# A hand-ordered rewrite of a gated attention and MLP backward pass: 4-byte transposes, long weight rows, program order

## The chip, the cores and the metric

The kernel runs on one core of a Trainium2 chip. The metric is the device time of one execution in microseconds (us). One execution of each kernel was also profiled. In what follows PE is TensorE (PEld are its weight loads), DVE is VectorE, ACT is ScalarE, POOL is GpSimd, SP is SyncE, which here issues the loads and, at the end, a few small stores. PEclk is the share of the full TensorE clock that was granted. L472 is a line of the kernel whose profile is being read, so the same operation has different line numbers in different kernels.

A run counts as slow if it is over 1.5% above the fastest of the same kernel, and the recorded ratios are formed from fast runs. The medians beside them are over all runs of a kernel. The profiled execution of the kernel before is not one of the listed ones: its span of 459.0 us is longer than that of every run of it that the record lists as fast (448 to 456 us), so small differences from its profile mean nothing.

## The reference, cut to what matters

The program computes a forward pass and all its gradients: a decode-size attention block (one query token, 32 heads, a cache of 4096 keys of 128 numbers) and a small MLP (640 to 1728 to 640), mixed by a sigmoid gate.

```python
q = (x @ wq).reshape(B, 1, 32, 128).transpose(0, 2, 1, 3)
scores = einsum("bhqd,bhkd->bhqk", q, k_cache) * 128 ** -0.5
p = softmax(scores)
o = einsum("bhqk,bhkd->bhqd", p, v_cache)
a = o.transpose(...).reshape(B, 1, 4096) @ wo
h = x @ w1 + b1;  b = (h * tanh(softplus(h))) @ w2
out = g * a + (1 - g) * b          # g = sigmoid(sum(x * gate_w))
# returned: out and the gradients of x, k_cache, v_cache, wq, wo, w1, b1, w2, gate_w
```

For each head the kernel reads 1 MB of K and 1 MB of V and writes 1 MB of dK and 1 MB of dV. dV is the outer product of p with the output gradient row, and dK is the outer product of ds with q, where `ds = p * (dp - sum(p * dp))` and dp is V times the output gradient. All in all about 165 MB pass between HBM and the chip. With only one query, the arithmetic is light: most of the work is to transpose K and V so that TensorE can multiply them, and to write the outer products.

## The kernel before: the parts that the argument touches

Each head transposes 32 blocks of K and 32 of V, 128x128 in bf16, eight to a PSUM tile, copies them out on ACT and multiplies them by a vector. The work is written head by head. A scheduler then orders the instructions of every engine, with `high_priority` marking the short dependent chain.

```python
def transposes(src, dst):
    for c in range(NTB):
        tp = tr_ps.tile([P, TB, P], BF16, name="tr", tag="tr")
        for t in range(TB):
            nc.tensor.transpose(tp[:, t, :], src[:, c * TB + t, :], ident_bf[:])
        nc.scalar.copy(...)                                  # 128x512 as float32
KT = kvT.tile([P, J, P], BF16, name="KT", tag="KT")
transposes(Kn, KT)
for j in range(J):
    nc.tensor.matmul(S[:, j:j + 1], lhsT=KT[:, j, :], rhs=gp["qTs_g"][:, hh:hh + 1], ...)
with hp():                                                   # tc.high_priority
    ...                                                      # max, exp, sum, 1/sum, p
... # the same for V, then ds, dq, o, and the outer products dV and dK
```

wo and wq are transposed on PE as well. wo rows are 1280 bytes, wq pieces 1024 bytes, and dwq is written group by group in 1024-byte pieces.

Of the kernel before, what the change touches and what calls it, by code (L numbers as in the profile page):

```python
# [8 lines left out]
ALU = mybir.AluOpType  # L9
# [7 lines left out]
def kernel(  # L17
# [29 lines left out]
    assert Dh == P and Sk % P == 0 and D % P == 0  # L47
    J = Sk // P
    RC = D // P
    G = 4 if H % 4 == 0 else (2 if H % 2 == 0 else 1)  # L50
    NG = H // G
    GD = G * Dh
    FP = 96
    assert F % FP == 0
    FCN = F // FP
    FCC = 3 if FCN % 3 == 0 else 1
    NCH = FCN // FCC
    FW = FCC * FP
    scale = float(Dh) ** -0.5
    TB = 8 if J % 8 == 0 else J  # L60
    NTB = J // TB
    JD = max(1, min(J - 1, int(round(J * 0.59)))) if J > 1 else J
# [7 lines left out]
    wo_v = A_wo.rearrange("(h d) n -> d h n", d=P)  # L70
    dwo_v = out_5.rearrange("(h d) n -> d h n", d=P)
    w1_v = B_w1.rearrange("(rc r) f -> r rc f", r=P)
    dw1_v = out_6.rearrange("(rc r) f -> r rc f", r=P)
    w2_v = B_w2.rearrange("(fc p) n -> p fc n", p=FP)
    dw2_v = out_8.rearrange("(fc p) n -> p fc n", p=FP)
    b1_row = B_b1.rearrange("(o f) -> o f", o=1)
    db1_rows = out_7.rearrange("(fc p) -> fc p", p=FP)
    x_row = A_x.rearrange("a b d -> (a b) d")
    x_rows = A_x.rearrange("a b (c p) -> (a b c) p", p=P)
    dy_row = grad_out.rearrange("a b d -> (a b) d")  # L80
    dy_rows = grad_out.rearrange("a b (c p) -> (a b c) p", p=P)
    gw_row = gate_w.rearrange("(o d) -> o d", o=1)
# [4 lines left out]

    const = ctx.enter_context(tc.tile_pool(name="const", bufs=1))
    KBUFS, VBUFS = 4, 4
    kv_in = ctx.enter_context(tc.tile_pool(name="kv_in", bufs=KBUFS))  # L90
    kvT = ctx.enter_context(tc.tile_pool(name="kvT", bufs=1))
    outs = ctx.enter_context(tc.tile_pool(name="outs", bufs=3))
    wts2 = ctx.enter_context(tc.tile_pool(name="wts2", bufs=2))
    wts1 = ctx.enter_context(tc.tile_pool(name="wts1", bufs=1))
    small = ctx.enter_context(tc.tile_pool(name="small", bufs=4))
    mlp1 = ctx.enter_context(tc.tile_pool(name="mlp1", bufs=1))
    tr_ps = ctx.enter_context(tc.tile_pool(name="tr_ps", bufs=2, space=PSUM))
    ss_ps = ctx.enter_context(tc.tile_pool(name="ss_ps", bufs=3, space=PSUM))
    grp_ps = ctx.enter_context(tc.tile_pool(name="grp_ps", bufs=2, space=PSUM))
    qd_ps = ctx.enter_context(tc.tile_pool(name="qd_ps", bufs=1, space=PSUM))  # L100
    HP = 1200
    LP = -200000

    def f32view(ap2d):
        return ap2d.bitcast(F32)

    ident_bf = const.tile([P, P], BF16, name="ident_bf")
    nc.gpsimd.memset(ident_bf[:], 0.0)
    nc.gpsimd.affine_select(
        out=ident_bf[:], in_=ident_bf[:], compare_op=ALU.not_equal, fill=1.0,  # L110
# [4 lines left out]
    ones_f = const.tile([P, P], F32, name="ones_f")  # L115
    nc.vector.memset(ones_f[:], 1.0)
    zeros_f = const.tile([P, 32], F32, name="zeros_f")
    nc.vector.memset(zeros_f[:], 0.0)
    warm = const.tile([P, 8], F32, name="warm")
    nc.gpsimd.tensor_tensor(warm[:], zeros_f[:, 0:8], zeros_f[:, 8:16], ALU.add)  # L120

    with tc.tile_pool(name="setup", bufs=1) as sp:
        vec_rows = sp.tile([3 * RC, P], BF16, name="vec_rows")
        nc.scalar.dma_start(vec_rows[0:RC, :], x_rows)
        nc.scalar.dma_start(vec_rows[RC:2 * RC, :], dy_rows)
        nc.scalar.dma_start(vec_rows[2 * RC:3 * RC, :], gw_rows)
        xg_bc = sp.tile([P, 2, D], BF16, name="xg_bc")
        nc.scalar.dma_start(xg_bc[:, 0, :], x_row.partition_broadcast(P))
        nc.scalar.dma_start(xg_bc[:, 1, :], gw_row.partition_broadcast(P))
        dy_bc = sp.tile([P, D], BF16, name="dy_bc")  # L130
        nc.scalar.dma_start(dy_bc[:], dy_row.partition_broadcast(P))

        cols_ps = grp_ps.tile([P, 3 * RC], BF16, name="cols_ps", tag="grp")
        nc.tensor.transpose(cols_ps[:], vec_rows[:], ident_bf[0:3 * RC, 0:3 * RC])
        cols_bf = const.tile([P, 3 * RC], BF16, name="cols_bf")
        nc.scalar.copy(cols_bf[:], cols_ps[:])
        cols_f = const.tile([P, 3 * RC], F32, name="cols_f")
        nc.vector.tensor_copy(cols_f[:], cols_ps[:])
        x_col_bf = cols_bf[:, 0:RC]
        x_col_f = cols_f[:, 0:RC]  # L140
        dy_col_f = cols_f[:, RC:2 * RC]
        gw_col_f = cols_f[:, 2 * RC:3 * RC]

        zprod = sp.tile([P, D], F32, name="zprod")
        nc.vector.tensor_tensor(zprod[:], xg_bc[:, 0, :], xg_bc[:, 1, :], ALU.mult)
        z_all = sp.tile([P, 1], F32, name="z_all")
        nc.vector.reduce_sum(z_all[:], zprod[:], axis=AX.X)
        en = sp.tile([P, 1], F32, name="en")
        nc.scalar.activation(en[:], z_all[:], ACT.Exp, scale=-1.0)
        den = sp.tile([P, 1], F32, name="den")  # L150
        nc.vector.tensor_tensor(den[:], en[:], ones_f[:, 0:1], ALU.add)
        g_raw = sp.tile([P, 1], F32, name="g_raw")
        nc.vector.reciprocal(g_raw[:], den[:])
        g_bf = sp.tile([P, 1], BF16, name="g_bf")
        nc.vector.tensor_copy(g_bf[:], g_raw[:])
        g_all = const.tile([P, 1], F32, name="g_all")
        nc.vector.tensor_copy(g_all[:], g_bf[:])
        omg_bf = sp.tile([P, 1], BF16, name="omg_bf")
        nc.vector.tensor_tensor(omg_bf[:], ones_f[:, 0:1], g_all[:], ALU.subtract)
        omg_all = const.tile([P, 1], F32, name="omg_all")  # L160
        nc.vector.tensor_copy(omg_all[:], omg_bf[:])

        da_col_bf = const.tile([P, RC], BF16, name="da_col_bf")
        nc.vector.tensor_tensor(da_col_bf[:], dy_col_f, g_all[:].to_broadcast([P, RC]), ALU.mult)
        db_col_bf = const.tile([P, RC], BF16, name="db_col_bf")
        nc.vector.tensor_tensor(db_col_bf[:], dy_col_f, omg_all[:].to_broadcast([P, RC]), ALU.mult)
        da_bc_bf = const.tile([P, D], BF16, name="da_bc_bf")
        nc.vector.tensor_tensor(da_bc_bf[:], dy_bc[:], g_all[:].to_broadcast([P, D]), ALU.mult)
        db_bc_bf = const.tile([P, D], BF16, name="db_bc_bf")
        nc.vector.tensor_tensor(db_bc_bf[:], dy_bc[:], omg_all[:].to_broadcast([P, D]), ALU.mult)  # L170

    aT_acc = const.tile([P, RC], F32, name="aT_acc")
    nc.vector.memset(aT_acc[:], 0.0)
    dxT_acc = const.tile([P, RC], F32, name="dxT_acc")
    nc.vector.memset(dxT_acc[:], 0.0)
    bT_acc = const.tile([P, RC], F32, name="bT_acc")
    nc.vector.memset(bT_acc[:], 0.0)

    def load_group(g):
        wq_g = wts2.tile([P, RC, GD], BF16, name="wq_g", tag="wq_g")  # L180
        nc.sync.dma_start(wq_g[:], wq_v[:, :, g * GD:(g + 1) * GD])
        wo_g = wts2.tile([P, G, D], BF16, name="wo_g", tag="wo_g")
        nc.sync.dma_start(wo_g[:], wo_v[:, g * G:(g + 1) * G, :])
        return wq_g, wo_g

    def transpose_blocks(dst3, blocks):
        n = len(blocks)
        i = 0
        while i < n:
            m = min(8, n - i)  # L190
            tp = grp_ps.tile([P, 8, P], BF16, name="wtr_ps", tag="grp")
            for t in range(m):
                nc.tensor.transpose(tp[:, t, :], blocks[i + t], ident_bf[:])  # L193
            nc.scalar.copy(
                f32view(dst3[:, i:i + m, :].rearrange("p a b -> p (a b)")),
                f32view(tp[:, 0:m, :].rearrange("p a b -> p (a b)")),
            )
            i += m

    def prep_group(g, wq_g, wo_g):  # L200
        qbc_ps = grp_ps.tile([P, GD], F32, name="qbc_ps", tag="grp")
        for rc in range(RC):
            nc.tensor.matmul(qbc_ps[:], lhsT=x_col_bf[:, rc:rc + 1].to_broadcast([P, P]),  # L203
                             rhs=wq_g[:, rc, :], start=(rc == 0), stop=(rc == RC - 1))
        qd_sb = wts2.tile([P, 2, GD], BF16, name="qd_sb", tag="qd_sb")
        nc.scalar.copy(qd_sb[:, 0, :], qbc_ps[:])
        qT_ps = grp_ps.tile([P, G, 2], BF16, name="qT_ps", tag="grp")
        for hh in range(G):
            nc.tensor.transpose(qT_ps[:, hh, 0:1], qd_sb[0:1, 0, hh * Dh:(hh + 1) * Dh], ident_bf[0:1, 0:1])
        qTs_g = wts2.tile([P, G], BF16, name="qTs_g", tag="qTs_g")  # L210
        nc.scalar.mul(qTs_g[:], qT_ps[:, :, 0], scale)
# [247 lines left out]
    for h in range(1, min(PRE_K, H)):  # L459
        load_k(h)  # L460
# [109 lines left out]
```

## Time and profile before

| quantity | before |
|---|---|
| time, median of 4 runs | 459.94 us (454.61 to 469.2) |
| profiled span | 459.0 us |
| PE busy | 382.5 us, 83% |
| data moved | 167.81 MB in 45560 packets |
| mean rate | 366 GB/s |

The first part of the page of the kernel before gives busy time, share of the span and the number of instructions of each engine:

```profile
span 459.0 us, 16426 instructions
PE 382.5 (83%) x7301; PEld 350.4 (76%) x7320; DVE 264.4 (58%) x693; ACT 248.5 (54%) x571; POOL 96.3 (21%) x109
```

The second part cuts the span in 40 equal slices. A digit is a tenth, 9 being 90% or more; the last row is the rate of data movement in each slice.

```profile
PE   0898989959899899969989599899999959999930
...
PEclk9998988859956699665987579587955879655555
DMA  8979999999999999999999999999999999973593
GB/s 248 427 308 349 411 425 417 413 416 334 418 422 360 369 360 363 420 354 406 420 418 370 386 386 375 420 406 394 413 424 419 364 348 347 416 284 127 206 365 118
```

PE and DMA are both near full nearly everywhere. Apart from a dip in slice 18, DMA falls off only in slices 36 to 38, counted from 1: the last K or V load landed at 405.3 us, in slice 36, and the last heads are still being computed. The same in a table of stretches (columns: length, busy us and instruction count per engine, granted clock, DMA share, GB/s), for the middle of the kernel:

```profile
60.00:400.00 340.00, 299.79 (x5779) 275.62 (x5792) 199.54 (x515) 195.65 (x449) 80.39 (x83) 0.75 1.01 392
```

The costliest PE groups are the bf16 transposes (columns: line, engine, operation, tiles, shape, count; busy us, mean ns of one; idle time before them and what ended it):

```profile
L254 PE MATMUL tr<-ident_bf,Kn 128*128 128x128 bf16 x1024 | 105.1, 250 | 3.8 <-issue 1.2
L254 PE MATMUL tr<-ident_bf,Vn 128*128 128x128 bf16 x1024 | 105.1, 256 | 3.9 <-ACT VT L255 3.2
```

The mean of 250 ns is latency, and matmuls are pipelined. What one costs in a stream is the time from the start of one to the start of the next. In the instruction records that step, between two transposes with no other matmul in between, is 107 ns in the median at the granted clock 0.50 (677 of them) and 55 ns at 1.00 (1062 of them).

### The profile page before, as it was taken

To read this page: it belongs to the slowest core of one execution; us is meant where nothing else is said; L and a number is where in the kernel's file an instruction comes from. 1 tells how busy PE (TensorE), PEld (TensorE's weight loads), DVE (VectorE), ACT (ScalarE), POOL (GpSimd) and SP (SyncE) were. 2 spreads that over 40 slices of the span, in tenths; PEclk is the share of its full clock that TensorE was granted. 3 is DMA by queue.
4 is the path that set the end of the run, shared out by engine and by line. 5 is a ranking of instruction groups with operands and counts; after the bars stand their busy time and mean duration, and the time that the engine had idled before them with its cause. 6 is when DMAs were issued, how large, how long until landed. Compare 5 with 4: busy or idle time off the path is not lost.

```text
span 459.0 us, 16426 instructions
## 1 busy us (share of the span) xinstructions
PE 382.5 (83%) x7301; PEld 350.4 (76%) x7320; DVE 264.4 (58%) x693; ACT 248.5 (54%) x571; POOL 96.3 (21%) x109
## 2 busy tenths in 40 slices
PE   0898989959899899969989599899999959999930
PEld 0688969838798788858888588887999858989820
DVE  0355735633627357737477488565656736665782
ACT  1575766626717777534665356656756536654510
POOL 0001010100100443551317141041000501014020
PEclk9998988859956699665987579587955879655555
DMA  8979999999999999999999999999999999973593
GB/s 248 427 308 349 411 425 417 413 416 334 418 422 360 369 360 363 420 354 406 420 418 370 386 386 375 420 406 394 413 424 419 364 348 347 416 284 127 206 365 118
DMA packets 45560, 167.81 MB, mean 366 GB/s; under 512 B 3122, under 2 KB 27506, under 8 KB 29106
## 3 DMA queue, kind: packets, MB, share of 16 engines
q1 hardware_dynamic: 25161, 84.24, 48.5%
q0 software_dynamic: 10368, 71.54, 38.0%
q10 hardware_dynamic: 9961, 10.99, 7.0%
q8 instruction: 57, 0.93, 0.8%
q14 instruction: 13, 0.11, 0.1%
HBM read 84.73 MB, written 82.03 MB: 363 GB/s over the span
## 4 chain that ended last, share of the span: by engine, by line
PE 61%; DMA 22%; ACT 7%; DVE 6%; issue 3%; ACTq 0%; SPq 0%; DVEq 0%
PE tr L254 25%; DMA wq_g<-in_A_wq_dram 10%; PE wtr_ps L193 6%; DMA wo_g<-in_A_wo_dram 5%; PE ss L298 5%; PE ss L285 5%; PE ss L303 5%; PE ss L263 4%; DMA w2c<-in_B_w_dram 3%; PE qbc_ps L203 3%; PE dobc_ps L217 2%; DMA xg_bc<-in_gate_w_dram 2%; PE ss L271 2%; ACT VT L255 2%; ACT KT L255 2%
## 5 line engine op out<-in xcount | busy, mean ns | idle before, releaser
L254 PE MATMUL tr<-ident_bf,Kn 128*128 128x128 bf16 x1024 | 105.1, 250 | 3.8 <-issue 1.2
L254 PE MATMUL tr<-ident_bf,Vn 128*128 128x128 bf16 x1024 | 105.1, 256 | 3.9 <-ACT VT L255 3.2
L255 ACT COPY VT<-tr 128x512 f32<-128x512 f32 x128 | 74.0, 583 | 53.0 <-PE tr L254 51.4
L255 ACT COPY KT<-tr 128x512 f32<-128x512 f32 x128 | 73.5, 585 | 42.3 <-PE tr L254 41.4
L254 PEld LDWEIGHTS <-Kn 128*128 128x128 bf16 x1024 | 81.0, 116 | 7.9 <-issue 6.1
L254 PEld LDWEIGHTS <-Vn 128*128 128x128 bf16 x1024 | 80.6, 117 | 5.9 <-issue 4.2
L324 DVE TENSOR_TENSOR dV_sb<-p_bf,qd_sb 128x2048 bf16<-128x2048 bf16 x64 | 80.6, 1264 | 4.8 <-ACT p_bf L280 4.8
L324 DVE TENSOR_TENSOR dK_sb<-ds_bf,qd_sb 128x2048 bf16<-128x2048 bf16 x64 | 78.5, 1229 | 0.3
L332 POOL DMA_DIRECT2D out_dram<-dV_sb x32 | 17.8, 555 | 164.4 <-DVE negD L293 80.4
L335 POOL DMA_DIRECT2D out_dram<-dK_sb x32 | 17.4, 544 | 144.5 <-DVE dK_sb L324 76.8
L263 PE MATMUL ss<-qTs_g,KT 128*128 128x1 bf16 x1024 | 40.9, 165 | 3.9 <-issue 2.1
L263 PEld LDWEIGHTS <-KT 128*128 128x128 bf16 x1024 | 37.3, 101 | 5.2 <-issue 3.0
L285 PEld LDWEIGHTS <-VT 128*128 128x128 bf16 x1024 | 34.1, 100 | 4.5 <-issue 2.3
L285 PE MATMUL ss<-doTs_g,VT 128*128 128x1 bf16 x1024 | 34.5, 164 | 2.1 <-ACT VT L255 1.1
L298 PEld LDWEIGHTS <-Kn 128*128 128x128 bf16 x1024 | 30.7, 99 | 6.6 <-issue 5.7
L298 PE MATMUL ss<-ds_bf,Kn 128*128 128x1 bf16 x1024 | 31.5, 164 | 4.6 <-issue 2.6
L303 PEld LDWEIGHTS <-Vn 128*128 128x128 bf16 x1024 | 31.2, 100 | 1.8 <-issue 1.4
L303 PE MATMUL ss<-e_bf,Vn 128*128 128x1 bf16 x1024 | 31.8, 164 | 0.7 <-issue 0.4
L347 DVE TENSOR_TENSOR dwq_g<-dqbc_ps,cols_f 128x512 bf16<-128x512 f32 x40 | 26.1, 682 | 5.6 <-DMA out_dram<-dwq_g 4.2
L203 PE MATMUL qbc_ps<-wq_g,cols_bf 128*128 128x512 bf16 x33 | 14.0, 535 | 16.2 <-DMA wq_g<-in_A_wq_dram 8.3
L273 DVE TENSOR_REDUCE negM<-ss 128x1 f32<-128x128 f32 x32 | 9.3, 290 | 30.9 <-PE ss L271 30.9
L278 DVE RECIPROCAL rz<-ss 128x1 f32<-128x1 f32 x32 | 5.4, 169 | 30.8 <-PE ss L276 30.8
(331 smaller groups left out, 522.2 us busy)
## 6 DMA issues: line engine op xcount, KB each, us to landing
Kn<-in_A_k_cache_dram SPq DMA_DIRECT2D x32, 1024.0 KB, 9.5
Vn<-in_A_v_cache_dram SPq DMA_DIRECT2D x32, 1024.0 KB, 16.1
out_dram<-dV_sb POOLq DMA_DIRECT2D x32, 1024.0 KB, 9.7
out_dram<-dK_sb POOLq DMA_DIRECT2D x32, 1024.0 KB, 10.2
wq_g<-in_A_wq_dram SPq DMA_DIRECT2D x8, 640.0 KB
wo_g<-in_A_wo_dram SPq DMA_DIRECT2D x8, 640.0 KB, 16.5
out_dram<-dwo_g ACTq DMA_DIRECT2D x8, 640.0 KB, 11.6
out_dram<-dwq_g ACTq DMA_DIRECT2D x8, 640.0 KB, 3.3
```

Source lines behind the costliest of these rows:

```text
L193: nc.tensor.transpose(tp[:, t, :], blocks[i + t], ident_bf[:])
L203: nc.tensor.matmul(qbc_ps[:], lhsT=x_col_bf[:, rc:rc + 1].to_broadcast([P, P]), rhs=wq_g[:, rc, :], start=(rc == 0), stop=(rc == RC - 1))
L254: nc.tensor.transpose(tp[:, t, :], src[:, c * TB + t, :], ident_bf[:])
L255: nc.scalar.copy(f32view(dst[:, c * TB:(c + 1) * TB, :].rearrange("p a b -> p (a b)")), f32view(tp[:].rearrange("p a b -> p (a b)")),)
L263: nc.tensor.matmul(S[:, j:j + 1], lhsT=KT[:, j, :], rhs=gp["qTs_g"][:, hh:hh + 1], start=True, stop=True)
L285: nc.tensor.matmul(DP[:, j:j + 1], lhsT=VT[:, j, :], rhs=gp["doTs_g"][:, hh:hh + 1], start=True, stop=True)
L298: nc.tensor.matmul(DQ[:, j:j + 1], lhsT=Kn[:, j, :], rhs=ds_bf[:, j, 0:1], start=True, stop=True)
L303: nc.tensor.matmul(OP[:, j:j + 1], lhsT=Vn[:, j, :], rhs=e_t[:, j:j + 1], start=True, stop=True)
L324: nc.vector.tensor_tensor(dst[:, a:b, :].rearrange("p j (a b) -> p j a b", b=2), colsrc[:, a:b, :].unsqueeze(2).to_broadcast([P, n, Dh // ...
L332: nc.gpsimd.dma_start(dVv[h], dV_sb[:])
L335: nc.gpsimd.dma_start(dKv[h], dK_sb[:])
L347: nc.vector.tensor_tensor(dwq_g[:, rc, :], dqbc_ps[:], x_col_f[:, rc:rc + 1].to_broadcast([P, GD]), ALU.mult)
```

## The change: its intent, and the diff

The rewrite has these aims: halve the number of transposes by moving two bf16 numbers as one 4-byte element; avoid the transposes of wo and wq; make the rows of weight transfers long; read w1 once; write dwq late, in 7 KB rows, when the end of the kernel has room for it; and fix the order of all instructions by hand. The last is one line, `tc.manual_schedule()`: every engine executes in the order in which the program is written.

```diff
-    wo_v = A_wo.rearrange("(h d) n -> d h n", d=P)
-    w2_v = B_w2.rearrange("(fc p) n -> p fc n", p=FP)
+    wo_v = A_wo.rearrange("(g p i) n -> g p i n", p=P, i=G)
+    w2_v = B_w2.rearrange("(p fc) n -> p fc n", p=FP)
...
+    ctx.enter_context(tc.manual_schedule())
...
+    def transposes(src, c):
+        tp = tr_ps.tile([P, 4, P], F32, name="tr", tag="tr")
+        flat = f32v(src[:].rearrange("p j d -> p (j d)"))
+        for t in range(4):
+            k = c * 4 + t
+            nc.tensor.transpose(tp[:, t, :], flat[:, k * P:(k + 1) * P], ident_f[:])
+        ... # one ACT copy, the same 128x512 float32
+    def products(out, tb, c, vec):     # even and odd halves of the pairs, accumulated
+        for t in range(4):
+            for par in range(2):
+                nc.tensor.matmul(out[:, 2*k:2*k+2], lhsT=tb[:, t, par, :], rhs=vec[:, par, :], ...)
...
+    # dot products of wo, wq, w1, w2 rows with a broadcast row, on DVE, in place of transposes
+    nc.vector.scalar_tensor_tensor(junk[:, 0:D], in0=wos[g][:, i, :], scalar=1.0, in1=da_bc[:],
+                                   op0=ALU.mult, op1=ALU.mult, accum_out=gp["do4"][:, i:i + 1])
...
+    for h in range(H):
+        load_k(h + 3); load_v(h + 3)   # ... (and, in the third head of a group, the next weights)
+        head_k(h)                      # K transposes, scores, their max
+        head_v(h)                      # max over partitions, exp, sum, V transposes, dp
+        if h > 0: side(q if q and hh > 1 else mq, 1)
+        head_o(h)                      # dV, part, o, ds
+        side(q if q and hh > 1 else mq, 1)
+        ...                            # in the last three heads: dwq, made on DVE
+        head_d(h)                      # dq, dK
+        ...                            # dwq stores; the side steps that finish a group
+        side(q if q else mq, 1)
```

`side` takes the next step from a queue of side work: preparing q and do of the next group of four heads, finishing a group (dwo, dx), and the MLP.

## The prediction

> **What bounds the kernel before.** Two things, nearly equal.
>
> - Data movement: 167.81 MB. The queue table adds up to 94% of the 459.0 us span (about 433 us). In the view of forty slices, those with only K/V rows move 413 to 427 GB/s, those with weights 334 to 370. The packet records say why: an 8192-byte packet takes 309 ns in the median (26.5 GB/s per engine), a 1280-byte one 59 ns on average (21.7), a 1024-byte one 48 ns (21.3). 29106 of 45560 packets are under 8 KB.
> - TensorE: the chain of waits is 61% PE, 25% of it the 128x128 transposes. In the timeline a bf16 transpose costs 108 ns at granted clock 0.50, about 59 at 1.00; a one-column product 29 and 24. At the low clock a head needs 64 x 108 + 128 x 29 ns = 10.7 us, plus about 1.2 us of float32 matmuls and 2.3 us of weight transposes: 14.2 us, against 459/32 = 14.3 us per head.
>
> Because PE is late, loads run ahead of stores and the end is starved: from 410 to 430 us, 111 to 120 GB/s with PE full at clock 0.50.
>
> **What the change does.**
>
> 1. K/V transposes as 4-byte pairs: 2048 become 1024 of the same width; the build shows one matmul for each. The Trainium skill, "TensorE: Matmul & The Clock Gate", Terms, gives trn2 a transpose mode 4x faster for FP32, so I assume one pass, bound by the weight load. The trace's float32 weight load takes 192 ns against about 100 for bf16: about 110 ns per pair (estimate). Saves about 3.4 us per head at the low clock. The PSUM copies stay (256 of 0.58 us). The products keep their number, with strided weights; I assume no cost.
> 2. The wo and wq transposes go (320), replaced by short products, column broadcasts and DVE multiply-reduces: saves about 1.5 us PE per head, adds about 2 us DVE (870 ns for each 640-wide reduce in the trace).
> 3. DMA: w1 read once (2.2 MB less), wo/dwo 5 KB rows, wq 2 KB, w2 7.5 KB, dwq 7 KB. About 20 us of DMA time disappear; with the 2.2 MB, 433 becomes about 405 us.
> 4. dwq is written last, filling the starved tail: 10 to 12 us less idle.
> 5. Strict program order: each head waits in turn for PE, ACT, DVE. I add up 3.7 us for K (ACT copies paced), 4.2 for V, 2.7 for part, second half of dV, ds and dq: 11 to 12 us, plus DVE side work. DMA needs 11.1 us per head (4.7 MB at 420 GB/s). So this loop is nearly equal to DMA.
>
> **Critical path.** PE work leaves it; DMA becomes the limit, the in-order loop close behind. 165.6 MB at 400 to 420 GB/s is 394 to 414 us, plus about 12 us of start and end, plus some stalls: **420 us**, 8 in 10 between **402 and 446**. Faster by over 2%: 0.90; within 2%: 0.05; slower: 0.05.
>
> **Signs.** Right: PE busy falls from 382.5 to roughly 270 us; packets under 25000; no starved stretch before the end; mean over 390 GB/s; the chain led by DMA or DVE, not transposes. Step 1 wrong: 4-byte transposes 200 ns or more apiece. Step 5 wrong: DMA share well under 0.9 mid-kernel with no engine over 85%.
>
> **What would make it wrong.** Float32 transposes in several passes (430 ns each would make PE slower than before)[...]; DVE side work delaying the max and so the whole head.

## The result, and the profile after

Ratios are the recorded ones, of mean times of fast runs, so they are not quite the ratios of the medians quoted beside them.

| quantity | before | after |
|---|---|---|
| time, median of 4 runs | 459.94 us | 565.84 us (564.09 to 569.45) |
| ratio to before | | 1.2501, 95% interval 1.236 to 1.2641 |
| PE busy | 382.5 us, 83% | 385.3 us, 68% |
| DVE busy | 264.4 us | 313.6 us |
| packets | 45560 | 26328 |
| mean rate | 366 GB/s | 292 GB/s |

The rewrite is 25% slower. It moves less data in fewer packets, and no engine and no queue is full. The busy times and the slices of the page after:

```profile
span 565.1 us, 13730 instructions
PE 385.3 (68%) x5916; PEld 337.2 (60%) x5916; DVE 313.6 (56%) x780; ACT 188.2 (33%) x410; POOL 46.4 (8%) x95
...
PE   2899776786668735787667655678668755777840
...
DMA  7995796699779976698784998669878975763493
GB/s 293 419 382 248 283 377 238 231 382 360 315 243 345 383 275 242 228 373 352 277 297 176 365 381 317 235 230 337 320 280 297 360 300 170 246 248 141 176 403 148
```

The middle as one stretch, with the same columns as before:

```profile
60.00:540.00 480.00, 337.55 (x5388) 294.11 (x5387) 278.43 (x673) 172.49 (x373) 40.22 (x75) 0.68 0.78 290
```

PE is busy 70% of it, DVE 58%, ACT 36%, and the DMA share is 0.78. This is what a chain of waits looks like: everything has slack, and still nothing goes faster. PE's idle time, span less busy, grew from 76.5 us to 179.8 us. The longest wait of SP is this:

```profile
SPq L116 <- PE sB L577: 350.3, 25, 24.4
```

That is the issue of a K load, which waited 350.3 us in all, 25 times, for the dq products (L577) of an earlier head to free the buffer. So loads wait for compute. That alone does not say that DMA is not the limit: in the kernel before, where DMA was full, K and V loads waited for PE too (`SPq L448 <- PE ss L298: 98.3, 12, 14.4` is the longest of five such waits, 268 us in all). The DMA share of 0.78 says it. The transposes of the page after:

```profile
L472 PE MATMUL tr<-ident_f,Kn 128*128 128x128 f32 x512 | 127.9, 416 | 0.0
...
L472 PE MATMUL tr<-ident_f,Vn 128*128 128x128 f32 x512 | 95.4, 320 | 0.0
```

Half as many, and 223.3 us busy in place of 210.2. In the records, one 4-byte transpose follows the other after 213 ns at the clock 0.50 (483 of them) and after 109 ns at 1.00 (292 of them): at either clock, twice the bf16 step. The products lose nothing by their strided weights: 27 and 25 ns, the same as in the kernel before.

What one head costs is best read from the chain of waits (columns: start us, length us, what). This is what matters of head 30 (heads count from 0), whose only side work, the making of dwq on DVE, comes after ds and so outside the chain:

```profile
515.65 1.81 PE tr L472 x8
517.46 0.20 PE sA L481 x8
517.66 0.96 PE tr L472 x4
...
519.85 0.59 ACT tT L474
...
520.85 0.51 PE tr L472 x4
521.44 0.60 ACT tT L474
...
523.80 0.44 issue
524.24 0.36 ACT p_bf L530
524.63 1.23 DVE dV_sb L536
525.85 0.11 DVE pj L554 x2
525.96 1.14 DVE dV_sb L536
527.10 0.28 DVE dj L563 x2
527.40 0.30 DVE ds_bf L565
527.74 0.99 PE sB L577 x32
528.73 0.32 PE tr L472
```

The K phase takes 5.20 us (515.65 to 520.85), the V phase 3.78, then DVE's dV, part and ds 3.11 while PE stands still but for the 32 o products, and dq 0.99: 13.08 us until the next head's first transpose. Nothing of the next head overlaps with it. Thirty-two such heads are 419 us. The first transpose starts at 15.6 us and the last dq ends near 543, 22 us before the end. So the bare chain alone gives about 456 us (15.6 + 419 + 22). The rest, about 109 us, lies in heads that are longer than this one, by side work and by the waits that it brings; not all of it is taken apart below. From the score maximum of head 2 (65.03 us) to that of head 31 (533.98 us) a head takes 16.2 us on average (468.95 / 29), 3.1 us more than the bare one. Some heads are far longer. One that carries both a dx and a preparation takes 24 us, from 190.34 to 214.25 us by the starts of two score maxima.

### The profile page after: what moved, and what is told of

The parts are those of the page before. It is cut to its first block, busy times and chain, and to the rows that moved or that the text cites. A ratio compares the mean times of both kernels' runs of the same rounds, so it can differ in the third digit from the quotient of the medians.

```text
span 565.1 us, 13730 instructions
## 1 busy us (share of the span) xinstructions
PE 385.3 (68%) x5916; PEld 337.2 (60%) x5916; DVE 313.6 (56%) x780; ACT 188.2 (33%) x410; POOL 46.4 (8%) x95
## 2 busy tenths in 40 slices
DMA packets 26328, 164.93 MB, mean 292 GB/s; under 512 B 2812, under 2 KB 2812, under 8 KB 10012
## 4 chain that ended last, share of the span: by engine, by line
PE 45%; DVE 36%; ACT 7%; issue 6%; DMA 4%; SPq 1%; ACTq 0%; DVEq 0%
PE tr L472 30%; DVE dV_sb L536 13%; ACT tT L474 6%; DVE dK_sb L536 6%; PE sA L481 4%; DMA w_sb<-in_B_w_dram 4%; DVE junk L253 4%; DVE junk L330 4%; PE h_ps L353 3%; PE sB L577 3%; PE sB L481 2%; DVE junk L414 2%; DVE dj L563 2%; DVE junk L450 1%; DVE ds_bf L565 1%
## 5 line engine op out<-in xcount | busy, mean ns | idle before, releaser
L474 ACT COPY tT<-tr 128x512 f32<-128x512 f32 x256 | 149.0, 586 | 152.9 <-PE tr L472 142.5
L472 PE MATMUL tr<-ident_f,Kn 128*128 128x128 f32 x512 | 127.9, 416 | 0.0
L481 PEld LDWEIGHTS <-tT 128*128 128x128 bf16 x2048 | 82.2, 103 | 65.5 <-ACT tT L474 58.9
L472 PE MATMUL tr<-ident_f,Vn 128*128 128x128 f32 x512 | 95.4, 320 | 0.0
L472 PEld LDWEIGHTS tr<-ident_f,Kn 128*128 128x128 f32 x512 | 94.3, 217 | 1.7 <-issue 1.6
L536 DVE TENSOR_TENSOR dV_sb<-p_bf,qd 128x2048 bf16<-128x2048 bf16 x64 | 78.1, 1221 | 18.5 <-ACT p_bf L530 18.5
L536 DVE TENSOR_TENSOR dK_sb<-ds_bf,qd 128x2048 bf16<-128x2048 bf16 x64 | 75.3, 1217 | 0.0
L472 PEld LDWEIGHTS tr<-ident_f,Vn 128*128 128x128 f32 x512 | 67.3, 164 | 0.0
L577 PEld LDWEIGHTS <-Kn 128*128 128x128 bf16 x1024 | 34.7, 107 | 43.6 <-issue 43.6
L577 PE MATMUL sB<-ds_bf,Kn 128*128 128x1 bf16 x1024 | 31.8, 165 | 36.7 <-DVE ds_bf L565 36.7
L559 PEld LDWEIGHTS <-Vn 128*128 128x128 bf16 x1024 | 28.2, 96 | 0.0
## 6 DMA issues: line engine op xcount, KB each, us to landing
out_dram<-dK_sb POOLq DMA_DIRECT2D x31, 1024.0 KB, 10.4
```

The source lines that it names most:

```text
L472: nc.tensor.transpose(tp[:, t, :], flat[:, k * P:(k + 1) * P], ident_f[:])
L474: nc.scalar.copy(sb[:].rearrange("p a b -> p (a b)"), tp[:].rearrange("p a b -> p (a b)"))
L481: nc.tensor.matmul(out[:, 2 * k:2 * k + 2], lhsT=tb[:, t, par, :], rhs=vec[:, par, :], start=(par == 0), stop=(par == 1))
L536: nc.vector.tensor_tensor(dst[:, a:b, :].rearrange("p j (a b) -> p j a b", b=2), col[:, a:b, :].unsqueeze(2).to_broadcast([P, n, Dh // 2, 2]),
L559: nc.tensor.matmul(O, lhsT=vts[h][:, j, :], rhs=st["e"][:, j:j + 1], start=(j == 0), stop=(j == J - 1))
L577: nc.tensor.matmul(DQ, lhsT=kts[h][:, j, :], rhs=st["ds"][:, j, 0:1], start=(j == 0), stop=(j == J - 1))
```

## The experiments

Theory A: the written order is the loss. Each engine executes strictly in program order, so one head's chain runs from end to end before the next begins, and side work placed in the chain lengthens it. Rival B: the 4-byte transposes are themselves what slows the kernel. Rival C: the added DVE work, the strided w1 loads or the DMA layout are the loss, whatever the order. Smaller rivals stand with their runs. Medians and ratios, all against the kernel before. There were e1 to e4 on chip 10, e5 to e9 on chip 13, e10 to e13 on chip 10 again, e14 and e15 on chip 12. Between calls, ratios compare better than medians. One caution for e1 to e4: their ratios take the kernel before at 458.3 us, a mean into which runs go that the record lists as slow. Against its three runs listed as fast (453.8 us) they would be 1.234, 1.010, 0.968 and 1.255; no reading below turns on it.

| run | median us | ratio to before | 95% interval |
|---|---|---|---|
| the change | 565.84 | 1.2501 | 1.236 to 1.2641 |
| e1_after_bf16tr | 560.56 | 1.2221 | 1.2114 to 1.2329 |
| e2_before_f32tr | 460.47 | 0.9991 | 0.9822 to 1.0161 |
| e3_after_scheduled | 440.36 | 0.9589 | 0.9476 to 0.9701 |
| e4_after_mlp_late | 569.45 | 1.2425 | 1.2318 to 1.2532 |
| e5_after_pipelined | 505.02 | 1.1119 | 1.1052 to 1.1186 |
| e6_after_thin_side (wrong results) | 531.83 | 1.1681 | 1.1556 to 1.1806 |
| e8_sched_short_rows | 452.01 | 0.9937 | 0.9862 to 1.0013 |
| e9_sched_w1_contig | 430.24 | 0.948 | 0.9416 to 0.9544 |
| e10_sched_prefetch2 | 468.38 | 1.0323 | 1.0253 to 1.0394 |
| e12_pipelined_thin_side (wrong results) | 479.91 | 1.0588 | 1.0528 to 1.0649 |
| e13_sched_pf2_dx_by_group | 470.41 | 1.0368 | 1.0296 to 1.044 |
| e14_sched_prefetch4 | 443.08 | 0.9767 | 0.97 to 0.9835 |
| e15_pipelined_thin_w1 (wrong results) | 470.42 | 1.0393 | 1.0317 to 1.0469 |

All others gave correct results.

### The 4-byte transposes, undone alone

```diff
-        tp = tr_ps.tile([P, 4, P], F32, name="tr", tag="tr")
-        for t in range(4):
-            nc.tensor.transpose(tp[:, t, :], flat[:, k * P:(k + 1) * P], ident_f[:])
+        tp = tr_ps.tile([P, 8, P], BF16, name="tr", tag="tr")
+        for t in range(8):
+            nc.tensor.transpose(tp[:, t, :], src[:, c * 8 + t, :], ident_bf[:])
     # products: one matmul of one column per block, with the plain q and do columns
```

> The changed kernel with its K and V transposes put back to 2048 bf16 blocks (step 1 of the prediction undone alone, order and all else kept). Theory A (the loss is the strict in-order loop; a 4-byte transpose takes about 213 ns at the low clock and 107 at full, twice a bf16 one, so step 1 neither saves nor costs TensorE time): 555 to 577 us. Rival B (the 4-byte form is itself what slows the kernel): below 520 us.

Measured: 560.56 us, within theory A's range; PE busy 377.6 us against 385.3. The pair form is not what slows the kernel. The bf16 steps in the records are again 107 and 56 ns.

### The 4-byte transposes, done alone in the kernel before

```diff
-                tp = tr_ps.tile([P, TB, P], BF16, name="tr", tag="tr")
-                for t in range(TB):
-                    nc.tensor.transpose(tp[:, t, :], src[:, c * TB + t, :], ident_bf[:])
+                tp = tr_ps.tile([P, TB // 2, P], F32, name="tr", tag="tr")
+                for t in range(TB // 2):
+                    nc.tensor.transpose(tp[:, t, :], flat[:, k * P:(k + 1) * P], ident_f[:])
     # and products over the two halves of the pairs
```

> The kernel before with 4-byte transposes and pair products alone (step 1 done alone). Theory A: transposes cost the same TensorE time per byte, so within 2% of before (450 to 470 us). Rival B (the pairs slow the kernel): above 480. My prediction's step 1 (110 ns a pair) would say about 420 to 440, with the DMA as the limit.

Measured: 460.47 us, ratio 0.9991. The line of its groups shows why nothing moved:

```profile
L271 PE MATMUL tr<-ident_f,Kn 128*128 128x128 f32 x512 | 106.2, 327 | 8.2 <-DVE ident_f L114 6.2 <-ACT KT L272 0.8 <-ACT VT L272 0.2
```

512 transposes of pairs keep PE busy 106.2 us, where 1024 of bf16 kept it busy 105.1. Step 1 of the prediction would have shown here, in a kernel whose PE is 83% busy, and did not. Rival B falls by both runs.

### The same program, ordered by the scheduler

```diff
-    ctx.enter_context(tc.manual_schedule())
```

> The changed kernel without the line that keeps program order, so that the scheduler orders the instructions again, as in the kernel before; same instructions, same buffers, same DMA. Theory A (order is the loss): 430 to 480 us, and PE waits between heads go. Rival C (the added DVE work, the strided w1 product or the DMA layout is the loss): above 540 us.

Measured: 440.36 us, in theory A's range. One line is worth 125 us (565.84 less 440.36), and the rewritten algebra under a scheduler is 3 to 4% faster than the kernel before. Its page:

```profile
span 436.0 us, 13764 instructions
PE 350.3 (80%) x5916; PEld 320.2 (73%) x5916; DVE 299.3 (69%) x780; ACT 184.5 (42%) x410; POOL 47.8 (11%) x95
...
DMA  7999899999999999989999889999999999984795
```

The same 5916 matmuls and 780 DVE instructions. PE's idle time is 85.7 us, not 179.8; its wait for ds before the dq products, 36.7 us in the change, is down to 8.8 (`PE sB L576 <- DVE ds_bf L564: 8.8, 6, 2.8`), because other work is done there: between the part-transpose at 213.90 us and the dq products at 214.95, for one, PE runs seven V transposes, which must be of another head. And DMA is at 90% or more nearly everywhere, which was the state that the prediction had forecast for the change. Rival C falls as the main cause, since all that it names is still in this kernel.

### The MLP held back: does PE wait for w1?

In the chain of waits of the change, a DMA of w1 stood as its longest single piece:

```profile
5.46 22.55 DMA w_sb<-in_B_w_dram
28.05 5.55 PE h_ps L353 x30
```

It was taken for a stall of 22.5 us, since the MLP is the first side step, in head 0.

```diff
-        side(q if q and hh > 1 else mq, 1)
+        side(q if q and hh > 1 else mq if h >= 4 else q, 1)      # and the two others alike
-        st = [h_part(0, 6), h_part(6, 12), h_part(12, 18), act1, act2]
+        st = [lambda: [h_part(i, i + 6)() for i in (0, 6, 12)], act1, act2]
```

> The changed kernel with its MLP side steps held back until head 4 (and the three parts of the w1 product joined to one step). Theory A: TensorE's 22.6 us wait for w1 in head 0 goes, the 16.5 us of strided w1 products stay: 540 to 552 us. Rival D (the wait only hides another start-up limit): no change, 562 to 570.

Measured: 569.45 us. The reading was wrong, and rival D stands: nothing was won. The chain gives a DMA's whole time from issue to landing to the DMA, although PE was busy for 14.2 of these 22.5 us, and for 10.6 of the last 12.4, after its first K transpose. What counts is the idle time of PE just before the product, in the groups:

```profile
L353 PE MATMUL h_ps<-cols_bf,w_sb 128*96 128x1 bf16 x90 | 16.6, 318 | 0.3 <-DMA w_sb<-in_B_w_dram 0.3
```

0.3 us. The same line shows a real cost: 90 products keep PE busy 16.6 us. Their step in the records is 180 ns, where the long w2 rows force the columns of w1 to be read with a stride of 18 elements; in the kernel before, the same 90, read without a stride, took 80 ns each. Held back, the 16 us simply fell into head 4.

### The next head's K phase written into the waits

```diff
+    k_chunks(0, 0, NT); k_max(0)
     for h in range(H):
-        head_k(h)
         head_v(h)
         ...   # head_o: dV, part, o
+        k_chunks(h + 1, 0, 2)          # before the part-transpose
         ...   # rest of head_o: ds; side work
+        k_chunks(h + 1, 2, NT)         # before dq
         head_d(h)
+        k_max(h + 1)
```

> The changed kernel, program order kept, but with the K phase (transposes, products, max) of the next head written into the waits of this head: half of it before the part-transpose, half before the dq product. Same instructions and buffers. Theory A (each head's chain runs alone because of the written order): 445 to 500 us, TensorE's idle time before the part and dq products mostly gone. Rival C (side work and strided loads, not the chain, make the period): above 530 us.

Measured: 505.02 us, 61 us less than the change, and 5 us above the upper end of theory A's range. PE's waits, as the changed kernel had them (columns: waited for; us in all, times, longest):

```profile
PE sB L577 <- DVE ds_bf L565: 36.7, 31, 1.4
PE sB L560 <- DVE pj L554: 29.9, 31, 2.0
PE o_ps L304 <- DVE om L299: 21.2, 8, 4.3
PE d_ps L102 <- DVE do4b L258: 18.1, 3, 7.2
```

The same view of this run:

```profile
PE sA L481 <- ACT tT L474: 17.2, 37, 0.6
PE sB L481 <- ACT tT L474: 17.1, 34, 0.6
PE d_ps L102 <- DVE m L276: 12.1, 2, 6.0
PE o_ps L304 <- DVE om L299: 9.5, 5, 2.6
```

The two waits inside the head's chain, 66.6 us in all, are down to 1.3 and 0.6 us, and what is left are waits of the side steps and of the copies. The same instructions in another order: the chain of one head is shown to be about half of the 125 us.

### The side work on DVE, thinned

```diff
-   in0=wos[g][:, i, :], ... in1=da_bc[:]
+   in0=wos[g][:, i, 0:8], ... in1=da_bc[:, 0:8]      # and the three others: wq, w2, w1 rows
```

> Wrong results on purpose: the changed kernel with its added DVE multiply-reduces over 8 columns in place of 640, 864 or 1024 (80 instructions, some 77 us of DVE busy time in the profile; about 60 us would go). DVE is busy 56% of the span, so by a mere count of busy time it should be free. Theory A (in the strict order the side work stands in the chain): 60 us less busy time gives 40 to 60 us back, 505 to 525 us. Rival E (the side work fits in DVE's idle time): above 550 us.

Measured: 531.83 us; DVE busy 251.9 us in place of 313.6, so 61.7 us of busy time less gave 34.0 us of time (565.84 less 531.83). That lies between the two ranges, 7 us above the upper end of theory A's. More than half of the time taken out had stood in the chain, although DVE was idle 44% of the span.

### Interleaved and thinned together, then w1 contiguous too

> Wrong results on purpose: the hand order with the next head's K phase in the waits (505 us) and the thinned DVE side work (which gave 34 us alone) together. If the two losses are independent: 505 less 34, 465 to 477 us. If the one hides the other: 490 us or more. If the strict order is all of the loss, with both mended it should come within 40 us of the scheduled form's 440.

Measured: 479.91 us, 3 us above the range for independent losses: 25 us on top of the 61. From the scheduled form it is 39.6 us by the medians and about 45 by the ratios, so the test "within 40 us" is neither passed nor failed.

```diff
-   lhsT=w1_sb[:, rc, :].rearrange("p (q c) -> p q c", c=FCN)[:, :, fc],
+   lhsT=w1_sb[:, rc, fc * FP:(fc + 1) * FP],        # wrong columns on purpose
```

> Wrong results on purpose: the hand order with the interleaved K phase and the thin DVE side work (480 us), and the w1 product also with contiguous weights (184 ns to about 81 ns for each of 90, as the traces of the two forms show). If the strided loads stand in the chain in full: 9 us less, 469 to 473 us. If they hide: 477 us or more.

Measured: 470.42 us, 9.5 us less (8.9 by the ratios), as 90 x (180 - 80) ns = 9.0 us says; 29 of the 90 ran at the clock 1.00 here, where they took 45 ns, so about 10 us. So the strided weight loads stood in the chain, as far as a difference between two calls can tell. Of the 125 us between the change and its scheduled form, 61 go with the interleaving, 25 with the DVE side work and 9.5 with the strided loads, though the scheduled form of 440 us still has the last two. About 30 us between 470 and 440 (36 by the ratios) are not taken apart. One thing differs that was not tested by itself: the granted clock was 0.594 here and 0.724 in the scheduled run, and each 4-byte transpose takes 213 ns at the half clock and 109 at the full. PE busy is 389.7 us here and 350.3 there, for the same number of matmuls. Why the clock was granted less is open.

### Row lengths, with DMA as the limit

```diff
-            nc.sync.dma_start(wos[g][:], wo_v[g])
+            for k in range(2):
+                nc.sync.dma_start(wos[g][:, k::2, :], wo_v[g][:, k::2, :])
     # dwo, w2, dw2 alike; wq in two halves of 512 columns
```

> The scheduled form of the changed kernel (the earlier run of 440 us), with the row lengths of before put back for wq (1 KB), wo, dwo, w2 and dw2 (1280 B), the same bytes and tiles. Step 3 of the prediction (long rows are worth DMA time, and DMA is the limit once the order is free): 448 to 458 us. Rival F (something else bounds the scheduled form): 436 to 445 us, the same.

Measured: 452.01 us against the scheduled form's 440.36, so 11.6 us, within the range for step 3; by the ratios 0.9937 against 0.9589. Its profile fell in a slow run, so its page is not compared. But packet sizes do not depend on that, and they show short packets in the loads alone (5824 of 1280 bytes, 5120 of 1024); dwo and dw2 stand there as 1408 packets of 5120 bytes. The edit also doubles the number of these transfers, and its fast runs were granted less clock (0.66 to 0.69, against 0.715 to 0.735). So 11.6 us is what the edit cost as a whole; that the row length is the cause is argued, not shown.

### The MLP rows mapped as before

```diff
-    w2_v = B_w2.rearrange("(p fc) n -> p fc n", p=FP)
+    w2_v = B_w2.rearrange("(fc p) n -> p fc n", p=FP)
-    lhsT=w1_sb[:, rc, :].rearrange("p (q c) -> p q c", c=FCN)[:, :, fc],
+    lhsT=w1_sb[:, rc, fc * FP:(fc + 1) * FP],
     # dw2, b1 and db1 follow; b1 and db1 are turned on PE
```

> The scheduled form with the MLP rows of w2, b1, db1 mapped as before (1280-byte rows), so that the w1 product loads contiguous weights. Correct results. A strided weight load cost 180 ns a matmul, a contiguous one about 30: 13 us of TensorE go, about 2 us of DMA come. Theory A (at the start TensorE is what loads and stores wait for): 428 to 437 us. If DMA alone bounds it: 440 to 444 us.

Measured: 430.24 us with correct results, the fastest version: 5.2% below the kernel before by the ratio. Against the scheduled form it is 10 us by the medians and 9 by the means of the fast runs (430.4 and 439.5), but 5 by the ratios, whose intervals overlap. Its w1 products step at 80 ns again, not at the "about 30" of the expectation, which holds for weights of 128 columns; so 9 us of PE go, and not 13. The 7.5 KB rows of w2 had cost more on PE than they had saved in DMA, and DMA alone did not bound the scheduled form. This version beats both kernels.

### The cushion of loads

> The 430 us version (scheduled, w1 contiguous) with K and V loaded two heads ahead (3 buffers each) and not three (4). In its profile the loads end near 376 us and the slices after that move 180 to 404 GB/s, because the last heads still have to be computed; two heads ahead should leave one head less to compute without loads: about one head's 10 us times the missing share of DMA there, so 422 to 429 us. Rival: the smaller cushion costs as much in the middle, 430 to 436 us.

```diff
-    KB, VB = 4, 4
+    KB, VB = 3, 3
-        load_k(h + 3); load_v(h + 3)
+        load_k(h + 2); load_v(h + 2)
```

Measured: 468.38 us, 38 us more, where less had been expected: my reading of the tail missed by far. The next run adds a shorter dx at the end:

> The prefetch-two version with the dx multiply-reduce done per group of four heads (512 columns) and not per two groups (1024), so that the last one, which stands at the end of the chain, is half as long (5 times 1.2 us become 5 times about 0.7): 2 to 3 us less than the prefetch-two run. Rival: the end waits for the last stores, and nothing changes.

Measured: 470.41 us, no gain; the intervals overlap. Its profile is of a fast run and shows what the missing buffer does. First PE's wait for K in the 430 us version, then in this one:

```profile
PE tr L478 <- DMA Kn<-in_A_k_cache_dram: 10.4, 2, 5.8
```

```profile
PE tr L476 <- DMA Kn<-in_A_k_cache_dram: 50.8, 12, 11.7
```

Two waits have become twelve and 10.4 us have become 50.8, which is the size of the loss. With this little cushion PE waits for data that arrives late, and the loads wait in turn for PE to free buffers (`SPq L115 <- PE sB L581: 132.3, 17, 17.5` is the longest such wait).

> The 430 us version with K and V loaded four heads ahead (5 buffers each) and 3 output buffers in place of 5 to make room. Prefetch two cost 38 us against three, with TensorE waiting 40 us for K loads in its profile, so the cushion of loads matters. If a deeper one still pays: 420 to 427 us. If three heads already cover the wait, or the fewer output buffers hold the stores back: 429 to 440 us.

Measured: 443.08 us, slower than with three. No wait of PE for K remained but 5.8 us at the start, but a new one stands in the list of waits: `DVE dK_sb L544 <- DMA out_dram<-dV_sb: 22.9, 5, 7.1`. DVE waits for an output buffer, of which there were three in place of five. That the output buffers are the cause is likely and not shown, since the run changed both. Three heads ahead with five output buffers is the best of the three that were tried.

## Why the prediction was wrong

The prediction said 420 us and 90% for faster; the change took 565.84 us. Point by point:

1. **"What bounds the kernel before"**: right. PE and DMA nearly equally full, and a starved end, are what the pages show.
2. **Step 1, "about 110 ns per pair (estimate)"**: wrong. It measured 213 ns at the low clock and 109 at the full one, against 107 and 55 for bf16, so a pair costs what two bf16 blocks cost. The estimate took the weight load for the bound, from 192 ns for a float32 weight load in an ordinary matmul against about 100 for bf16. Sorted by clock, the records of the kernel before have 189 ns against 97 at the clock 1.00 and 333 to 337 against 151 at 0.50: about twice as long at either clock, so the factor of two stood in the prediction's own figures, which were those of the full clock, and 110 ns at the low clock does not follow from them. The prediction's own sign for this, 200 ns or more apiece, appeared. The Trainium skill ("TensorE: Matmul & The Clock Gate", Terms) gives a transpose mode 4x faster for FP32. One matmul instruction per pair does run here, but no run measures a 4-byte transpose without that mode, and "4x faster" was no ground for "as fast as a bf16 block". PE busy stayed at 385.3 us where roughly 270 was forecast. The error alone did not slow the kernel, as the first two experiments show.
3. **Step 2, DVE work in place of PE transposes**: right in kind. DVE's busy time rose by 49 us. That it would stand in the chain was named among the dangers ("DVE side work delaying the max") and then not counted.
4. **Step 3, long rows**: right in kind, and mis-sized by the MLP. The packets fell from 45560 to 26328, where under 25000 was forecast. Putting short rows back in the loads cost 11.6 us, with the reservations above. The long w2 rows made w1's weights strided, which cost 9 to 10 us of PE; the prediction assumed no cost for strided weights, which held for a stride of 2 elements and failed for 18.
5. **Step 4, dwq last fills the tail**: not seen. Slices 34 to 38 after still move 141 to 248 GB/s. The 7 KB stores of dwq ran from 536.3 to 555.6 us, behind this starved stretch and not in it.
6. **Step 5, "11 to 12 us, plus DVE side work"**: this is the step that failed, and it decided the sign. A bare head takes 13.08 us, not 11 to 12: the K phase 5.20 us where 3.7 was added up (the transposes at twice the assumed step), V 3.78 where 4.2 was, and the first half of dV, 1.2 us, stands in the chain beside the second. Then the heads are 3.1 us longer on average than the bare one. The second is the larger miss: the bare chain alone would make about 456 us, the time of the kernel before, and the other 109 us lie in the heads made longer than that. The prediction found that this loop was "nearly equal to DMA" even so, and still took DMA as the limit with "some stalls" on top. Two limits of the same size, of which one is a chain with work put into it, are no ground for 90%. What it had not asked is what the kernel before does about the same chain. There the scheduler lets heads overlap, and the changed kernel gives that up in one line. The third experiment shows 125 us for that line. With it removed, the kernel takes 440 us, inside the predicted range of 402 to 446, and its DMA is full, as predicted. That is partly luck: PE is then busy 350.3 us, not roughly 270, and taking 8 us of PE work away made the kernel faster, so DMA was not the only limit.

The sign for step 5, a "DMA share well under 0.9 mid-kernel with no engine over 85%", is what the profile shows: 0.78, with PE at 70%.

The Trainium skill says of the engines' queues ("TensorE: Matmul & The Clock Gate", Part 1, Engine queue depths) that PE may pull weight loads ahead of matmuls in flight and that ACT and DVE are strictly first in, first out. The trace of the change agrees on PE: in head 30 the first weight load of the dq products ran at 526.02 us and its matmul only at 527.74, when ds was there. The dq products waited 36.7 us for ds in all, and no transpose of the next head passed them. On ACT and DVE no run here tests it.

## What to carry to other kernels

Before fixing an order by hand, add up the bare dependent chain of one iteration and all work that is written into it, and compare the sum with the period of the present kernel: if the scheduler now overlaps iterations, program order must be software-pipelined or it loses that overlap. An element twice as wide is not half the cost until its step is read from a trace at both clocks. In a chain of waits, a transfer's length is not idle time: read the idle time of the engine in front of the instruction that used it before moving anything.

## What the Trainium skill lacked or had wrong

- "TensorE: Matmul & The Clock Gate" (Terms; Part 4: PE-mode transpose) has no cost for a 4-byte transpose beside a 2-byte one. Here it is twice: 213 against 107 ns per 128x128 block at the clock 0.50, 109 against 55 ns at 1.00.
- The same page (Part 4) says that the full clock does not engage for transposes and gives about 275 ns in context. Here 1062 of 1739 measured bf16 transpose steps of the kernel before fell in stretches of granted clock 1.00, at 55 ns in the median, among other matmuls; the 250 ns of its profile are the recorded latency, not the step.
- "SBUF — State Buffer" (the note on 16-byte cachelines) lets bf16 stride up to 8 elements free. The runs agree and add sizes for weight loads: stride 2 costs 27 and 25 ns as contiguous does, stride 18 costs 180 ns for 96 columns, at both clocks, against 80 contiguous at the clock 0.50. The 80 ns is what "TensorE: Matmul & The Clock Gate" (LDWEIGHTS) gives, columns divided by 1.2; the page does not say that it falls with the clock, and at 1.00 the step was 45 ns (29 products of the last pipelined run).
- "DMA: Bandwidth & Descriptors" (Specifications) puts the smallest transfer for line rate at 512 bytes. Here, in the kernel before, 1280-byte packets move 23.3 GB/s per engine in the median and 21.7 on average, 8192-byte ones 26.5 and 25.2.
- No page warns that program order on several engines gives up the overlap of iterations that a scheduler finds: 125 us of 565 here.
